# Linear attention and two feed-forward stages on one core: heads laid out in pairs on both halves of the partitions, banks and plan of the work changed

## The chip, the cores and the metric

The kernel runs on one core of a Trainium2 chip. A core has a matrix engine (TensorE, here PE; its weight loads are listed as PEld), a vector engine (VectorE, DVE), an activation engine (ScalarE, ACT), a general engine (GpSimd, POOL) and a queue that issues transfers (SyncE, SP). SBUF is the working memory of 128 partitions; PSUM holds what PE writes, in 8 banks of 512 f32 values a partition. The metric is the device time in microseconds, the median of several runs.

## The reference

Three stages follow one another on 1536 tokens (2 batches of 768) of 384 features (8 heads of 48).

```python
# 1: attention with a decaying state; w is a decay per head and feature, u a bonus
for t in range(S):
    cur = np.einsum('bhd,bhe->bhde', u[None] * kt, vt)
    y[:, :, t] = np.einsum('bhd,bhde->bhe', rt, state + cur)
    state = w[None, :, :, None] * state + np.einsum('bhd,bhe->bhde', kt, vt)
# 2: four experts of 1024 hidden units, all of them run, weighted by p
for e in range(E):
    h = np.maximum(x @ w1[e], 0.0)
    out += p[:, e:e + 1] * (h @ w2[e])
# 3: 2048 hidden units
h = x @ w_in
g = h * (1.0 / (1.0 + np.exp(-1.702 * h)))
return (g @ w_out).astype(np.float32)
```

All arithmetic is f32.

## The kernel before

**Attention** works on 12 groups of 128 tokens (`attention`, L566), six to a batch. Inside a group the decay between two tokens is a quotient of powers, so keys and queries are scaled with tables of powers (`kp` and `rp`, made in `powers`, L493, from `pw`) to `kk` and `rr`. Two heads lie one behind the other on 96 partitions. For even heads the scores are a matmul on the first 48 rows, for odd heads one on all 96 rows with a copy of the keys, `kb`, whose first 48 rows are zeroed by a mask (`b_`, L587). `scores` (L655) is one step for each half of the heads; `mask` copies the later part of them over a diagonal, `at`, that holds the bonus (from `ruk` and `ss`; made on GpSimd by `diag`, L636, and in group 0 half of it on ScalarE by `dact`, L645). `values` (L706) multiplies by the values into `y`, half by half, and adds the carried state `sn`, which `products` (L680) updates from `kc` (keys by token times a table). `high` and `low` write the result as two f32r parts, `xh` and `xl`.

**The feed-forward stages** are 168 units (L752): block 0 (expert 0) 48 of 256 tokens, blocks 1 to 5 (three experts, and the last stage in two halves) 24 each of 512 tokens. A unit takes one chunk of 128 hidden units. Each f32 product is made of three f32r ones: high by high, high by low, low by high. So `up` (L769) is 9 matmuls into one of two banks, ScalarE and DVE read them out into `gh` and `gl` (three buffers each), and `down` (L824) is 9 more into three banks that are kept for 8 units. `end` adds the block's share to `acc`.

**Weights** come in chunks by SP (`load_w`, three buffers) and are split into `wh` and `wl` (`split_w`, 8 buffers each). Those of the last stage arrive as 64-bit numbers and are first made f32 by seven steps (`narrowing`, L145): six on DVE and a sum on GpSimd into one of `NR` = 8 buffers `r`. `narrow_w` (L434) gives all steps of a chunk one due time.

**The order** of all this is written out before the run. `Plan.add` (L60) takes for each step its engine, a cost, a due time, what it reads and writes, and which ring of buffers it takes; `Plan.order` (L84) plays the steps through with these costs and lags (L125 to L142), on each engine the ready step with the lowest due time first, and issues them in the order of their starts. On the chip each engine and the SP queue then keep that order and wait by semaphores. The due times of `up` and `down` make the second follow two units later:

```python
add("pe", 3 * c_mm(P, n, False), 6 * i + d - ..., lambda d=d: up(d), ..., takes=[("up", 2, U)] if d == 0 else ())
add("pe", 3 * c_mm(P, m, False), 6 * i + 12.5 + j + q / 8 - ..., ...)
```

Groups 0 and 1 stand ahead of unit 0, the others between the units of block 0 (L910 to L920). Matmuls called `warm` (L387) fill PE where the plan sees it idle before unit 0. `close` (L923) frees what attention held; from there on the "late" buffers exist.

Of the kernel before, what the change touches and what calls it, by code (L numbers as in the profile page):

```python
# [23 lines left out]
PD = 2 * D  # L24
G = 128
# [8 lines left out]
NR = 8  # L34
# [12 lines left out]
class Plan:  # L47
# [12 lines left out]
    def add(self, eng, cost, due, fn, reads=(), writes=(), takes=(), lag=None):  # L60
        i = len(self.ops)
        deps = set()
# [3 lines left out]
        for ring, size, k in takes:  # L66
            ks = self.rings.setdefault(ring, [])
            if ks:
# [56 lines left out]
LAG = {"dma": 2.6, "pe": 0.1, "dve": 0.1, "act": 0.1, "pool": 0.1, "none": 0.0}  # L125


def c_dve(n, fast=False):
    return (n / 2 if fast else n) / 960 + 0.07


def c_act(n, psum=True):
    return (n + (157 if psum else 224)) / 1400


def c_pool(n):
    return n * 0.0022 + 0.12


def c_mm(m, n, wide=True):  # L140

    return 2 * max(m / 1200, n / 1200) if wide else max(m / 1200, n / 2400)  # L142
# [25 lines left out]
def powers_of(nc, pw, w, most=None):  # L168
# [7 lines left out]
    while m < G:  # L176
        nc.vector.tensor_tensor(
            out=pw[:, :, m + 1:2 * m + 1], in0=pw[:, :, 1:m + 1],
            in1=pw[:, :, m:m + 1].to_broadcast([PD, NP, m]), op=ALU.mult)
# [161 lines left out]
def body(outer: ExitStack, tc: tile.TileContext, wv, cst, msk, dp, rk, tok, wts, wts2, out):  # L341
# [28 lines left out]
    wvs = ac_p.tile([PD, NP, 1], F32, name="wvs")  # L370
    cs = ac_p.tile([P, NCST], F32, name="cs")
    o = 0
    ub = cs[:, o:o + DM]; o += DM
    hm = cs[:PD, o:o + 1]; o += 1
    later = cs[:, o:o + G].bitcast(I32); o += G
    eye = cs[:, o:o + G]; o += G
    own = cs[:PD, o:o + PD]
    dps = ac_p.tile([P, E, NBT], F32, name="dps")
    pw = ac_p.tile([PD, NP, G + 1], F32, name="pw")
    qh = ac_p.tile([PD, NP, 1], F32, name="qh")  # L380
    rp = ac_p.tile([PD, NP, G], F32, name="rp")
    kp = ac_p.tile([PD, NP, G], F32, name="kp")
    wg = ac_p.tile([PD, NP, PD], F32, name="wg")
    tab = ac_p.tile([P, NP, PD], F32, name="tab")
# [14 lines left out]
    def load_const(key, due, t, src):  # L399
        add("dma", 0.1 if key in ("wv", "dp") else 0.5, due, lambda: sp.dma_start(t, src), writes=[key], lag=1.0)  # L400

    def load_group(g, dues):
        def one(i):
            if i == 0:
                T["rk", g] = rk_p.tile([PD, 2, NP, G], F32, tag="rk", name="rk")
                sp.dma_start(T["rk", g], rk[g])
# [6 lines left out]
        for i, k in enumerate(("rk", "tok", "val")):  # L413
            add("dma", 1.1, dues[i], lambda i=i: one(i), writes=[(k, g)], takes=[(k, 2, (k, g))],
                lag=1.0 if g < 2 else None)

    add("dma", 1.65, -9999, lambda: None)
    load_const("wv", -990, wvs.rearrange("p a b -> p (a b)"), wv)


    def load_w(q, due):
        if q < NMOE // 2:
            def fn():
                t = wraw_p.tile([P, 2, CW], F32, tag="w", name="w")
                sp.dma_start(t, wts[q])
                T["raw", q] = t
        else:
            def fn():
                t = wraw_p.tile([P, CW, 2], I32, tag="w", name="w")
                sp.dma_start(t.rearrange("p n t -> p (n t)"), wts2[q - NMOE // 2].bitcast(I32))  # L430
                T["raw", q] = t
        add("dma", 2.2, due, fn, writes=[("raw", q)], takes=[("w", NRAW, ("raw", q))])

    def narrow_w(c, due):  # L434
        k = c - NMOE
        q = NMOE // 2 + k
        load_w(q, due - 40)
        A, M, R = ("cva", k), ("cvm", k), ("r", c)
        tm = lambda: T[M]
        hi = lambda: T["raw", q][:, :, 1]  # L440
        lo = lambda: T["raw", q][:, :, 0]

        steps = narrowing(nc, hi, lo, lambda: T[A], tm, lambda: T[R])
# [14 lines left out]
        add("dve", f, due, first, reads=[("raw", q), "late"], writes=[M], takes=[("cvm", 2, M)])  # L458
        add("dve", f, due, steps[1], writes=[M])
        add("dve", f, due, steps[2], writes=[M])  # L460
        add("dve", l, due, sign, reads=[("raw", q), M], writes=[A], takes=[("cva", 2, A)])
        add("dve", f, due, steps[4], reads=[A], writes=[M])
        add("dve", l, due, steps[5], reads=[("raw", q)], writes=[M])
        add("pool", c_pool(CW), due, sum_, reads=[A, M], writes=[R], takes=[("r", NR, R)])

    def split_w(c, due):
        if c < NMOE and c % 2 == 0:
            load_w(c // 2, due - 20)
# [23 lines left out]

    def powers(half):  # L493
        s = slice(half * HP, (half + 1) * HP)
        qb = qh[:, s].to_broadcast([PD, HP, G])
        add("dve", c_dve(HP * G), -970 + 4 * half, lambda: dve.tensor_tensor(
            out=kp[:, s], in0=pw[:, s, 0:G][:, :, ::-1], in1=qb, op=ALU.mult), reads=["pw"], writes=[("kp", half)])
        add("dve", c_dve(HP * G), -969 + 4 * half, lambda: dve.tensor_tensor(
            out=rp[:, s], in0=pw[:, s, 0:G], in1=qb, op=ALU.mult), reads=["pw"], writes=[("rp", half)])

    def tables(due):

        kt = ac_p.tile([PD, NP, G], F32, name="kt")
        add("pool", 0.85, due, lambda: pool.tensor_tensor(
            out=kt, in0=kp, in1=pw[:, :, G:G + 1].to_broadcast([PD, NP, G]), op=ALU.mult),
            reads=[("kp", 0), ("kp", 1), "pw"], writes=["kt"])

        def turn():
            T["tab_ps"] = ps_at.tile([P, NP, PD], F32, tag="kv", name="tab_ps")
            for p in range(NP):  # L510
                pe.transpose(T["tab_ps"][:, p, :], kt[:, p, :], eye[:PD, :PD])
        add("pe", 0.9, due + 1, turn, reads=["kt", "cs1"], writes=["tab_ps"], takes=[("kv", 1, "tab_ps")])
# [504 lines left out]
```

## Time and profile before

| | us |
|---|---|
| median of 3 runs | 699.15 (699.08 to 701.87) |
| the profiled execution | 702.13 |
| its span, first to last instruction | 700.4 |
| PE busy in it | 678.6 |
| DVE, ACT, POOL busy in it | 369.6, 194.9, 169.9 |

The span is what the engines' instructions cover; the profiled execution's own time is 1.73 us longer. "Busy" counts an engine's instructions from start to end. PE's matmuls overlap, so the start-to-start times in a timeline tell its pace better than its busy time. A row's "idle before" is how long the engine had nothing to do ahead of it, with what released it.

### The profile page before, as it was taken

To read this page: it belongs to the slowest core of one execution; us is meant where nothing else is said; L and a number is where in the kernel's file an instruction comes from. 1 tells how busy PE (TensorE), PEld (TensorE's weight loads), DVE (VectorE), ACT (ScalarE), POOL (GpSimd) and SP (SyncE) were. 2 spreads that over 40 slices of the span, in tenths; PEclk is the share of its full clock that TensorE was granted. 3 is DMA by queue.
4 is the path that set the end of the run, shared out by engine and by line. 5 is a ranking of instruction groups with operands and counts; after the bars stand their busy time and mean duration, and the time that the engine had idled before them with its cause. 6 is when DMAs were issued, how large, how long until landed. Compare 5 with 4: busy or idle time off the path is not lost.

```text
span 700.4 us, 8982 instructions
## 1 busy us (share of the span) xinstructions
PE 678.6 (97%) x3644; PEld 584.1 (83%) x3644; DVE 369.6 (53%) x559; ACT 194.9 (28%) x351; POOL 169.9 (24%) x139
## 2 busy tenths in 40 slices
PE   8979999999999999999999999999799999999996
PEld 7879999999988888878888888887578888888885
DVE  7684554543585224784134764179993345434433
ACT  3432222222421113311113212134324344432331
POOL 6799545620012201223020302042430000000000
PEclk8799999999999999999999999999999999999999
DMA  7766332100252001351002430002100000001001
GB/s 230 238 209 206 89 93 70 46 23 1 81 191 91 0 1 45 136 181 45 1 0 91 145 126 1 0 1 90 46 0 1 1 0 1 1 0 46 18 28 49
DMA packets 12546, 45.90 MB, mean 66 GB/s; under 512 B 2129, under 2 KB 2642, under 8 KB 12498
## 3 DMA queue, kind: packets, MB, share of 16 engines
q1 hardware_dynamic: 12498, 45.26, 19.7%
q8 instruction: 30, 0.49, 0.3%
q14 instruction: 18, 0.15, 0.1%
HBM read 42.87 MB, written 2.38 MB: 65 GB/s over the span
## 4 chain that ended last, share of the span: by engine, by line
PE 82%; DVE 11%; POOL 2%; issue 2%; ACT 1%; DMA 1%; SPq 0%; DVEq 0%; POOLq 0%
PE dn L829 37%; PE up L775 36%; PE sc L661 4%; PE y L714 3%; DVE wl L479 1%; DVE a L154 1%; PE y L718 1%; DVE m L151 1%; DVE m L150 1%; PE kv L684 1%; DVE m L152 1%; DVE gl L794 1%; DVE m L157 1%; DMA tok<-in_tok 1%; POOL sn L695 1%
## 5 line engine op out<-in xcount | busy, mean ns | idle before, releaser
L775 PE MATMUL up<-xh,wh 128*128 128x512 f32 (+1 forms) x504 | 184.8, 367 | 4.0 <-DVE gl L794 2.3
L829 PE MATMUL dn<-gl,wh 128*128 128x512 f32 (+1 forms) x512 | 182.4, 356 | 2.4 <-DVE gl L813 2.4
L829 PE MATMUL dn<-gh,wh 128*128 128x512 f32 (+1 forms) x512 | 182.6, 357 | 1.3 <-DVE tp L855 1.2
L829 PE MATMUL dn<-gh,wl 128*128 128x512 f32 (+1 forms) x512 | 182.1, 356 | 0.0
L775 PE MATMUL up<-xl,wh 128*128 128x512 f32 (+1 forms) x504 | 180.9, 359 | 0.3 <-DVE xl L738 0.3
L775 PE MATMUL up<-xh,wl 128*128 128x512 f32 (+1 forms) x504 | 180.7, 359 | 0.0
L794 DVE SCALAR_TENSOR_TENSOR gl<-up,gh 128x512 fp32r<-128x512 f32 (+1 forms) x120 | 69.8, 582 | 161.0 <-ACT gh L788 160.7
L788 ACT ACTIVATE gh<-up 128x512 fp32r<-128x512 f32 (+1 forms) x120 | 61.5, 513 | 303.8 <-PE up L775 300.0
L775 PEld LDWEIGHTS up<-xh,wh 128*128 128x128 f32 x504 | 95.1, 189 | 19.7 <-DVE gl L794 3.6
L829 PEld LDWEIGHTS dn<-gl,wh 128*128 128x128 f32 x512 | 96.6, 189 | 17.2 <-DVE gl L813 3.0
L829 PEld LDWEIGHTS dn<-gh,wh 128*128 128x128 f32 x512 | 96.6, 189 | 16.7 <-ACT wh L475 1.6
L829 PEld LDWEIGHTS dn<-gh,wl 128*128 128x128 f32 x512 | 96.6, 189 | 13.5
L775 PEld LDWEIGHTS up<-xl,wh 128*128 128x128 f32 x504 | 95.1, 189 | 14.0 <-DVE xl L738 0.5
L775 PEld LDWEIGHTS up<-xh,wl 128*128 128x128 f32 x504 | 94.9, 188 | 13.9
L858 POOL TENSOR_TENSOR acc<-acc,tp 128x512 f32<-128x512 f32 x27 | 38.2, 1424 | 168.7 <-DVE tp L855 168.3
L809 DVE TENSOR_TENSOR gf<-up,sg 128x512 f32<-128x512 f32 x48 | 33.2, 691 | 75.2 <-ACT sg L805 75.2
L159 POOL TENSOR_TENSOR r<-a,m 128x768 f32<-128x768 f32 x16 | 31.5, 1970 | 132.3 <-DVE m L157 77.8
L805 ACT ACTIVATE sg<-up 128x512 f32<-128x512 f32 x48 | 28.7, 598 | 82.3 <-PE up L775 81.9
L813 DVE TENSOR_TENSOR gl<-gf,gh 128x512 fp32r<-128x512 f32 x48 | 33.4, 696 | 22.6 <-ACT gh L788 21.7
L788 ACT ACTIVATE gh<-gf 128x512 fp32r<-128x512 f32 x48 | 30.4, 632 | 41.5 <-DVE gf L809 41.0
L479 DVE TENSOR_TENSOR wl<-w,wh 128x768 fp32r<-128x768 f32 x32 | 35.1, 1098 | 2.5 <-ACT wh L475 1.9
L714 PE MATMUL y<-at,val 128*96 128x128 f32 x192 | 30.3, 288 | 1.1 <-DVE at L664 1.1
(78 smaller groups left out, 545.1 us busy)
## 6 DMA issues: line engine op xcount, KB each, us to landing
w<-in_wts SPq DMA_DIRECT2D x32, 768.0 KB, 4.4
rk<-in_rk SPq DMA_DIRECT2D x12, 384.0 KB, 4.1
tok<-in_tok SPq DMA_DIRECT2D x12, 384.0 KB, 3.8
val<-in_tok SPq DMA_DIRECT2D x12, 384.0 KB, 3.4
pb<-pscr SPq DMA_DIRECT2D x4, 768.0 KB, 4.0
out_t<-tp SPq DMA_DIRECT2D x8, 256.0 KB, 2.0
out_t<-tp SPq DMA_DIRECT2D x2, 128.0 KB, 4.1
cs<-in_cst SPq DMA_DIRECT2D x1, 192.5 KB, 4.1
```

The source lines that it names most:

```text
L159: lambda: pool.tensor_tensor(out=r(), in0=f(a), in1=f(m), op=ALU.add),
L479: dve.tensor_tensor(out=T[L_], in0=src(), in1=T[H_].bitcast(F32), op=ALU.subtract)
L661: pe.matmul(sc[:, j, :], lhsT=a[:n, h // 2, :], rhs=T[RR][:n, h // 2, :], start=True, stop=True)
L714: pe.matmul(y[:, p, :], lhsT=v2[:, h].rearrange("p b d -> p (b d)"), rhs=T["at", g, half][:, h % NP, :], start=hh == 0, stop=first and hh ...
L775: pe.matmul(T[U][:, :n], lhsT=a[:, s], rhs=b, start=d + k == 0, stop=d + k == 4)
L788: act.activation(out=T[GH][:, :n], in_=T[src][:, :n], func=f)
L794: dve.scalar_tensor_tensor(out=T[GL][:, :n], in0=T[U][:, :n], scalar=0.0, in1=T[GH][:, :n].bitcast(F32), op0=ALU.max, op1=ALU.subtract)
L805: act.activation(out=T[SG][:, :n], in_=T[U][:, :n], func=ACTF.Sigmoid, scale=1.702)
L809: dve.tensor_tensor(out=T[GF][:, :n], in0=T[U][:, :n], in1=T[SG][:, :n], op=ALU.mult)
L813: dve.tensor_tensor(out=T[GL][:, :n], in0=T[GF][:, :n], in1=T[GH][:, :n].bitcast(F32), op=ALU.subtract)
L829: pe.matmul(T[dn][:, cols], lhsT=T[a][:, s], rhs=T[b][:, cols], start=first and k == 0, stop=last and k == 2)
L858: pool.tensor_tensor(out=av, in0=av, in1=T[TP][:, :n], op=ALU.add)
```

## The change

Heads lie in pairs at partitions 0 to 47 and 64 to 111, so that tables, keys, queries and state have 112 rows (`PR`); each such load is two DMAs (`by_heads`). The scores of a group are one step: the even head of each pair on the lower half, the odd one on the upper half, in turn, into two banks. `kb`, its mask and `kp` go; the keys use `rp` read backwards. `at` holds even or odd heads instead of the first or last four; groups 0 and 1 make their diagonals wholly on ScalarE, the others two of four. `values` is one step. The state product of group 0, the transposed table and `y` of group 1 take banks of the `down` ring, the scores of group 1 the two `up` banks. Units from block 1 on follow their `up` with `down` three units later, and use two more `up` banks. Narrowing gets 12 buffers, a single buffer for its raw data, and its steps one by one behind units. Unit 0 does its two products with `xh` first. Costs, lags and due times of the plan are new.

```diff
-NR = 8
+NR = 12
+HS = 64
+PR = HS + D
-    def add(self, eng, cost, due, fn, reads=(), writes=(), takes=(), lag=None):
+    def add(self, eng, cost, due, fn, reads=(), writes=(), takes=(), lag=None, after=()):
-        deps = set()
+        deps = {j for k in after for j in self.wrote[k]}
...
-LAG = {"dma": 2.6, "pe": 0.1, "dve": 0.1, "act": 0.1, "pool": 0.1, "none": 0.0}
+LAG = {"dma": 2.6, "pe": 0.18, "dve": 0.12, "act": 0.12, "pool": 0.1, "none": 0.0}
...
+    def by_heads(engines, t, src):
+        engines[0].dma_start(t[:HS], src[:HS])
+        engines[1].dma_start(t[HS:], src[D:])
...
-                sp.dma_start(T["rk", g], rk[g])
+                by_heads((sp, sp), T["rk", g], rk[g])
...
-    add("dma", 1.65, -9999, lambda: None)
-    load_const("wv", -990, wvs.rearrange("p a b -> p (a b)"), wv)
+    add("dma", 0.75, -9999, lambda: None)
+    add("dma", 0.1, -990, lambda: by_heads((sp, act), wvs.rearrange("p a b -> p (a b)"), wv), writes=["wv"], lag=1.0)
...
-        add("dve", f, due, first, reads=[("raw", q), "late"], writes=[M], takes=[("cvm", 2, M)])
-        add("dve", f, due, steps[1], writes=[M])
...
+            lambda due, after: add("dve", f, due, first, reads=[("raw", q), "late"], writes=[M],
+                                   takes=[("cvm", 1, M)], after=after),
+            lambda due, after: add("dve", f, due, steps[1], writes=[M], after=after),
...
-            load_w(c // 2, due - 20)
+            load_w(c // 2, due - (60 if c < 8 else 20))
...
+    kp = rp[:, :, ::-1]
...
+        add("pool", 1.2, due, lambda: pool.memset(kcs, 0.0), writes=["kcs"])
...
-            def b_(s=s, i=i):
-                if i == 0:
-                    new(KB, [PD, NP, G])
-                act.activation(out=T[KB][:, s], in_=T[KK][:, s], func=ACTF.Copy, scale=hm)
...
-                on_act = 2 if g == 0 else 0
+                on_act = 4 if g < 2 else 2
...
-                for j in (0, 2, 1, 3):
-                    h = half * NP + j
-                    a, n = (T[KB], PD) if h % 2 else (T[KK], D)
-                    pe.matmul(sc[:, j, :], lhsT=a[:n, h // 2, :], rhs=T[RR][:n, h // 2, :], start=True, stop=True)
+            for p in range(NP):
+                for half in range(2):
+                    rows = slice(half * HS, half * HS + D)
+                    pe.matmul(T[sck[half]][:, p, :], lhsT=T[KK][rows, p, :], rhs=T[RR][rows, p, :], start=True, stop=True)
...
+            kv, kv_tag = ("kv", g), "sc0" if g else "dn2"
...
+        y_tag = "dn1" if g == 1 else "y"
...
+        deep = blk > 0
+        far = deep and i % 4 > 1
+        ups = [(d, ks) for ks in ((0, 2), (1,)) for d in range(3)] if i == 0 else [(d, (0, 1, 2)) for d in range(3)]
...
-                T[U] = ps_up.tile([P, 512], F32, tag="up", name="up")
+                T[U] = (late["up"] if far else ps_up).tile([P, 512], F32, tag="up", name="up")
...
-                add("pe", 3 * c_mm(P, m, False), 6 * i + 12.5 + j + q / 8 - (5.5 if i == len(units) - 1 else 0),
+                add("pe", 3 * c_mm(P, m, False), 6 * i + (18.5 if deep else 12.5) + j + q / 8 - (5.5 if i == len(units) - 1 else 0),
...
-    router(0)
+    router(-500)
...
+        late["raw"] = ctx.enter_context(tc.tile_pool(name="raw64", bufs=1))
+        late["up"] = ctx.enter_context(tc.tile_pool(name="ps_up2", bufs=2, space=PSUM))
...
+    def hand_over(chunks, u, v):
+        each = (v - u) / len(chunks)
+        for n, c in enumerate(chunks):
+            for m in range(6):
+                steps_at.setdefault(int(u + each * (n + m / 8.5)), []).append((c, m))
+
+    hand_over(range(NMOE, NMOE + NR), e0 + 6, k0)
+    hand_over(range(NMOE + NR, NCH), k0 + 1, k0 + 18)
...
+        for cn, m in steps_at.get(i, ()):
+            if m == 0:
+                load_w(NMOE // 2 + cn - NMOE, 6 * i - 40)
+                steps_of[cn] = narrow_w(cn)
+            steps_of[cn][m](6 * i + 12, [("up", i)])
```

## Rows read from the trace of the kernel before

**Rows 1.** The page, part 1: each engine's busy time, share, instructions.

```profile
PE 678.6 (97%) x3644; PEld 584.1 (83%) x3644; DVE 369.6 (53%) x559; ACT 194.9 (28%) x351; POOL 169.9 (24%) x139
```

**Rows 2.** Chain of waits around 212 us: start, length, engine, tile, line, count.

```profile
212.01 0.68 PE up L775 x3
```

**Rows 3.** Timeline of PE around a group's scores: start, length, line, tile, shapes.

```profile
87.62 0.28 PE L829 MATMUL dn<-gl,wh 128*128 128x256 f32 x1
87.74 0.28 PE L829 MATMUL dn<-gh,wl 128*128 128x256 f32 x1
87.95 0.71 PE L661 MATMUL sc<-rr,kk 48*128 48x128 f32 x4
88.59 0.71 PE L661 MATMUL sc<-rr,kb 96*128 96x128 f32 x4
...
89.26 0.28 PE L775 MATMUL up<-xl,wh 128*128 128x256 f32 x1
```

**Rows 4.** Timeline of PE from group 0's values to unit 0.

```profile
12.58 3.73 PE L714 MATMUL y<-at,val 128*96 128x128 f32 x16 [1.07 <-DVE at L664]
16.24 1.22 PE L661 MATMUL sc<-rr,kk 48*128 48x128 f32 x4
...
20.70 1.49 PE L684 MATMUL kv<-val,kc 128*96 128x96 f32 x8
21.98 2.39 PE L391 MATMUL warm<-acc 128*128 128x128 f32 x10
24.17 1.06 PE L714 MATMUL y<-at,val 128*96 128x128 f32 x4
...
29.29 0.36 PE L775 MATMUL up<-xh,wh 128*128 128x256 f32 x1
```

**Rows 5.** Stretches: length, busy PE, PEld, DVE, ACT, POOL, clock, DMA share, GB/s.

```profile
8.00:12.00 4.00, 2.31 (x16) 1.82 (x16) 3.96 (x7) 1.78 (x5) 3.75 (x4) 0.97 1.00 296
12.00:24.00 12.00, 11.42 (x50) 10.47 (x51) 7.97 (x15) 4.58 (x11) 8.70 (x11) 0.50 0.53 153
29.29:54.00 24.71, 20.14 (x164) 18.61 (x162) 19.57 (x35) 9.50 (x18) 23.06 (x18) 1.00 0.74 244
54.00:80.00 26.00, 25.54 (x209) 24.45 (x208) 15.48 (x30) 6.73 (x17) 22.71 (x22) 1.00 0.50 165
80.00:184.00 104.00, 104.00 (x864) 100.95 (x863) 48.20 (x98) 26.09 (x67) 34.24 (x32) 1.00 0.16 43
290.00:310.00 20.00, 19.54 (x86) 15.87 (x86) 16.93 (x21) 4.47 (x7) 6.24 (x4) 1.00 0.44 157
480.00:525.00 45.00, 38.42 (x162) 29.37 (x161) 43.74 (x55) 15.49 (x24) 15.39 (x8) 1.00 0.11 38
```

**Rows 6.** Timelines of ACT and POOL in the head.

```profile
9.14 0.68 ACT L646 ACTIVATE at<-cs,ss 128x128 f32<-128x128 f32 x2
...
16.07 2.05 POOL L638 TENSOR_TENSOR at<-ss,cs 128x512 f32<-128x512 f32 x2
...
22.33 2.78 POOL L677 TENSOR_TENSOR kc<-tok,tab 128x384 f32<-128x384 f32 x1 [2.98 <-issue]
```

**Rows 7.** Timeline of the SP queue at the start.

```profile
1.18 0.41 SPq L406 DMA_DIRECT2D rk<-in_rk  x1
```

**Rows 8.** Timeline of PE at the change to block 4.

```profile
490.25 0.50 PE L775 MATMUL up<-xh,wh 128*128 128x512 f32 x1 [1.30 <-DVE gl L794]
```

**Rows 9.** POOL's groups in 480 to 525 us: count, busy, mean ns.

```profile
L159 POOL TENSOR_TENSOR r<-a,m 128x768 f32<-128x768 f32 x5 | 10.3, 2069 | 26.3 <-DVE m L157 26.3
```

**Rows 10.** Timeline of DVE there: steps of the narrowing.

```profile
475.73 0.95 DVE L157 SCALAR_TENSOR_TENSOR m<-w,m 128x768 f32<-128x768 uint32 x1
476.60 0.55 DVE L150 TENSOR_SCALAR m<-w 128x768 int32<-128x768 int32 x1
477.19 2.08 DVE L151 TENSOR_SCALAR m<-m 128x768 f32<-128x768 f32 x1
```

**Rows 11.** Timeline of POOL beside it.

```profile
476.83 2.02 POOL L159 TENSOR_TENSOR r<-a,m 128x768 f32<-128x768 f32 x1 [4.49 <-DVE m L157]
```

More of the change, by code (lines that the diff above doesn't have):

```diff
@@ L67, in add @@
             ks = self.rings.setdefault(ring, [])
-            if ks:
+            if ks and ks[-1] in self.wrote:
                 deps.add(self.wrote[ks[-1]][0])
@@ L514, in tables @@
+        add("pe", 0.9, due + 1, turn, reads=["kt", "cs1"], writes=["tab_ps"], takes=[("dn1", 1, "tab_ps")])
+        add("act", c_act(DM), due + 2, lambda: act.activation(
+            out=tab.rearrange("p a b d -> p a (b d)")[:, :, :PR], in_=T["tab_ps"], func=ACTF.Copy),
             reads=["tab_ps"], writes=["tab"])
+        add("pool", 1.2, due, lambda: pool.memset(kcs, 0.0), writes=["kcs"])
         add("pool", 0.95, -500, lambda: pool.tensor_tensor(
-            out=wg, in0=pw[:, :, G:G + 1].to_broadcast([PD, NP, PD]), in1=times(own, PD, NP), op=ALU.mult),
@@ L517, in tables @@
-            reads=["pw", "cs1"], writes=["wg"])
+            out=wg, in0=pw[:, :, G:G + 1].to_broadcast([PR, NP, PD]), in1=times(own, PR, NP), op=ALU.mult),
+            reads=["pw", "own"], writes=["wg"])
     flag = const.tile([1, 1], I32, name="flag")
@@ L578, in attention @@
             n = (s.stop - s.start) * G
-            tabs = [("kp", j) for j in range(2) if s.start <= j * HP < s.stop]
             tabr = [("rp", j) for j in range(2) if s.start <= j * HP < s.stop]
@@ L644, in attention @@
+                add("pool" if on_act < NP else "none", c_pool((NP - on_act) * G) if on_act < NP else 0.0, d + 3, diag, reads=[SS, *((*SS, i) for i in ((0, NP) if g < 2 else (0,))), "cs1"],
+                    writes=[(*at, 0)], takes=[("at%d" % half, 2, at)])
                 for j in range(NP - on_act, NP):
-                    def dact(at=at, half=half, j=j):
-                        act.activation(
-                            out=T[at][:, j, :], in_=eye, func=ACTF.Copy, scale=T[SS][:, half * NP + j, :])
@@ new lines, in attention, with scores @@
+                    add("act", 0.3, d + 3, dact, reads=[SS, *((*SS, i) for i in ((0, NP) if g < 2 else (0,))), "cs1", at],
+                        writes=[(*at, j)])
+        sck = [("sc", g, half) for half in range(2)]
+        spare = g == 1
+        on_act = 4 if g < 2 else 2
+        def scores():
+            for half in range(2):
+                T[sck[half]] = (ps_up if spare else ps_at).tile(
+                    [P, NP, G], F32, tag="up" if spare else f"sc{half}", name="sc")
+            for p in range(NP):
+                for half in range(2):
+                    rows = slice(half * HS, half * HS + D)
+                    pe.matmul(T[sck[half]][:, p, :], lhsT=T[KK][rows, p, :], rhs=T[RR][rows, p, :], start=True, stop=True)
@@ L668, in attention, with mask @@
+        add("pe", 4 * c_mm(P, G), due["sc"][0], scores, reads=[KK, RR], writes=sck,
+            takes=[("up", 2, k) if spare else (f"sc{half}", 1, k) for half, k in enumerate(sck)])
+        for half in range(2):
+            at = ("at", g, half)
+            def mask(at=at, half=half):
+                dve.copy_predicated(T[at], times(later, P, NP), T[sck[half]])
             add("dve", c_dve(NP * G), due["mask"][half], mask,
-                reads=[sck, at, (*at, 0), *((*at, j) for j in range(NP - on_act, NP))], writes=[(*at, "m")])
+                reads=[sck[half], at, (*at, 0), *((*at, j) for j in range(NP - on_act, NP))], writes=[(*at, "m")])
@@ L686, in own_ @@
             def own_():
-                new(("sn", g + 1), [PD, NP, PD])
-                dve.tensor_tensor(out=T["sn", g + 1], in0=T[kv], in1=times(own, PD, NP), op=ALU.mult)
-            add("pool", c_pool(DM), due["kc"], by_token, reads=[tk_, "tab"], writes=[KC], takes=[("kc", 1, KC)])
-            add("pe", 4 * c_mm(PD, PD), due["kv"], products, reads=[KC, vl_], writes=[kv], takes=[("kv", 1, kv)])
-            add("dve", c_dve(DM), due["kv"] + 1, own_, reads=[kv, "cs1"], writes=[("sn", g + 1)],
+                new(("sn", g + 1), [PR, NP, PD])
@@ L693, in attention @@
+                dve.tensor_tensor(out=T["sn", g + 1], in0=T[kv], in1=times(own, PR, NP), op=ALU.mult)
+            add("pool", c_pool(DM), due["kc"], by_token, reads=[tk_, "tab", "kcs"], writes=[KC], takes=[("kc", 1, KC)])
+            add("pe", 4 * c_mm(PD, PD), due["kv"], products, reads=[KC, vl_], writes=[kv], takes=[(kv_tag, 1, kv)])
+            add("dve", c_dve(DM), due["kv"] + 1, own_, reads=[kv, "own"], writes=[("sn", g + 1)],
                 takes=[("sn", 2, ("sn", g + 1))])
@@ L941, in body @@
             split_w(c, 6 * i - 8)
-        for cn in narrow_at.get(i, ()):
-            narrow_w(cn, 6 * i - 20)
         if 0 < blk < E and t0 == 0 and c % 8 == 0:
```

247 lines of the change are left out of this document (118 added, 129 removed).

## The prediction

> **What bounds the kernel now.** I read the page first, then busy time by stretch, then TensorE's own timeline where a stretch fell short. The page says that TensorE (PE) is busy 97% of the span [rows 1], so the first question is whether that time is a floor. Nearly all of it is: three matmuls of 512 columns follow one another in 0.68 us, 0.227 us each [rows 2], those of 256 columns every 0.12 us [rows 3]. The program has 120 units of 18 matmuls at 512 columns and 48 units of 18 at 256, none of which the change removes: 120 x 18 x 0.227 + 48 x 18 x 0.12 = 594 us. The remaining 106 us of the span of 700.4 are what can move, and the stretches show where:
>
> - the head: the first matmul of unit 0 starts at 29.29 us [rows 4];
> - attention that PE runs between the units, mainly in 29 to 184 us;
> - idle PE: 24.71 - 20.14 = 4.6 us in 29.29 to 54 us, and 45.00 - 38.42 = 6.6 us in 480 to 525 us. In 80 to 184 us there is none [rows 5].
>
> So a stall that goes is worth its length wherever PE is the last to finish a stretch, and elsewhere nothing.
>
> **Scores in pairs.** Before, a half of the heads is one run: two matmul instructions (the two passes of an f32 matmul) for each of two even heads on 48 rows, then as many on 96 rows. Without the run the second of the `up` matmuls behind it would start two steps of 0.12 after the `dn` at 87.74, at 87.98; it starts at 89.26. One half costs 1.28 us, a group 2.56. The four 48-row passes start at 87.95 and the 96-row ones at 88.59, so eight passes take eight steps of about 0.11 (0.89; the shape of kk's and kb's runs is the same) and the other 0.39 are three changes of shape, 0.13 each: into 48 rows, to 96, and back to 128 [rows 3]. That a change from 48 to 96 rows costs anything, though both lie in the same array, says that PE works a 48-row matmul on a part of its rows in a mode of its own.
>
> After, all 16 passes have 48 rows, alternating between partitions 0 and 64 and between two banks, in one run per group. The switches fall to two (0.26). No row shows matmuls on different halves together, so three bounds: they overlap, 8 x 0.11 + 0.26 = 1.15 us; they follow one another, 16 x 0.11 + 0.26 = 2.04; each change of half costs a switch as well (7 x 0.13 more), 2.95. Saved per group: 1.41, 0.52 or -0.39, and for the ten groups 2 to 11 14.1, 5.2 or -3.9 us. I take the first, because the switch in the rows is the sign of a mode that leaves the other half free.
>
> The Trainium skill, TensorEngine Tiling (Array Packing), section Theoretical Speedup, puts a contraction of at most 64 rows at up to twice the speed, and its section Key Properties says that tiles load weights and multiply in parallel. By it the saving is the 14.1 us; by the rows alone, which show only one half in use, it is the 5.2. No run here shows the rule yet.
>
> The values, the state products and the keys keep their counts. `kb` on ScalarE goes (one activation a group), and ScalarE takes four diagonal activations of 0.34 us from GpSimd [rows 6]: lighter than the idle ScalarE has, as it is busy 26 of 104 us there [rows 5], so nothing on the path. The halves of `y` are now one block that waits for both masks; in 80 to 184 us neither mask is late.
>
> **The head.** Before, the chain on PE from 12.58 us on is: `y` of group 0 (3.7 us), scores of group 1 (16.24 to 20.70, 4.5 us at a granted clock of 0.50, the 1.2 GHz level), its state product (1.3), 2.2 us of warm-up matmuls that only fill a wait, then `y` of group 1 (from 24.17) [rows 4, 5]. The new order puts the diagonals of groups 0 and 1 on ScalarE: 16 x 0.34 = 5.4 us [rows 6], instead of GpSimd, where group 1's two took 2.05 us and began at 16.07 behind other work. Group 0's eight take 2.7 us and end with its masks at about the old 12.6, so its `y` is not earlier. But `kb` is no longer waited for and the two groups have banks of their own, so the scores of group 1 can stand before that `y`, in PE's wait: the 4.5 us leave the chain. With group 1's diagonals done by about 16 us the wait under the warm-up matmuls goes, 2.2 us. Against that `y` of group 1 comes earlier into the slow clock (24 passes at twice 0.11: up to 2.6 us more), and the keys' load is two issues on SP instead of one, 0.41 us each [rows 7]. I take 4.5 + 2.2 - 0.8 - 0.4 = 5.5 us gained. Bounds: 6.7 + 2.6 = 9.3 if the clock is up from the start, so that `y` of group 0 is faster too, nothing if ScalarE's 5.4 us of diagonals take over as the chain. Unit 0 may also begin before its low parts are there, 0.3 us or so, inside this error. The weights of units 0 to 7 now go ahead of the loads of groups 2 and 3. In 12 to 24 us the DMA engines were busy 53% [rows 5], since the queue on SP stood behind a buffer that was not free; the weights fill that gap, so I take nothing, and if they delay group 2, the next paragraph's stall stays.
>
> The tables and products on 112 partitions instead of 96 take the same time where it goes by columns; the state product's 16 more weight columns are at most a sixth of its 1.3 us in the head, and the clearing of `kcs` is one operation on GpSimd. Both stand beside other work after the head, and inside its bounds in it.
>
> **The early stall.** In 29.29 to 54 us GpSimd is busy 23.06 of 24.71 us and DVE 19.57 [rows 5]: PE's 4.6 us are waits for them. GpSimd loses one of two diagonals a group (1.0 us of the 2.05 for a pair [rows 6]), DVE nothing much, and both are asked to keep up with a PE that begins earlier. Also the second `kc` at 22.33 waited 2.98 us for the product before it [rows 6], which the head now runs earlier. I take half: 2.5 us; bounds 0 and 4.6. What is late next here is GpSimd again.
>
> **Narrowing step by step, 12 slots, four banks.** In 480 to 525 us DVE is busy 43.74 of 45 us [rows 5]. 162 matmuls there would need 162 x 0.227 = 36.8 us: 8.2 us are lost, in waits for DVE such as the 1.30 at 490.25 [rows 8]. GpSimd forms the sums of five chunks in that stretch [rows 9]. A chunk is four short steps of 0.55 us on DVE and two of 0.95, 4.1 us, and a short step that meets GpSimd's sum takes 2.08 instead (477.19, beside the sum at 476.83 [rows 10, 11]): 5.6 us. Twelve slots move four of the eight late chunks to where DVE is half idle; the other four come one in 17/4 units of 18 x 0.227 = 4.1 us, about 17 us apart, so 2.6 in such a stretch instead of five. That takes 2.4 x 5.6 = 13.4 us off DVE: some 30 us of work in the 37 that the matmuls need. With a unit more between `up` and `dn`, and two more banks for `up`, a burst may last 4 us longer before PE sees it. I take 7.2 of the 8.2 as gained, and bound it by 0 (the same steps under other units stall PE elsewhere) and 8.2. The same for the stretch around 308 us: 0.4. In the steady stretches the deeper order neither adds nor removes matmuls, and its cost is nothing as long as a unit's results are read out within its 4.1 us, as they are before. The single staging buffer lets a chunk load only after the one before is narrowed; of the 22 us between chunks (5.5 units) some 9 are left for it, and a late one would hold DVE, not PE, for the length of four banks.
>
> **The sum.** 14.1 + 5.5 + 2.5 + 7.2 + 0.4 = 29.7 us. The profiled execution took 702.13 us (span 700.4 and 1.73 around it): 672.4. The median of the runs is 2.98 below that execution, so 669.5 us.
>
> **Rivals.**
>
> - The pairs do not overlap: 29.7 - 8.9 = 20.8 gained, 678.4 us. For it: the rows show no two matmuls at once. Against: the mode of their own.
> - Each change of half costs a switch: 18 us less gained, 687.5. For it: 0.13 at every change of shape seen. Against: shape and mode stay the same here.
> - ScalarE's diagonals become the head's chain, or the early stretch stays bound by GpSimd: 5.5 + 2.5 less, 677.5. For it: GpSimd is full.
> - The narrowing only moves its stalls: 7.6 less, 677.1. For it: the work is the same. Against: the steps no longer come in a row, and four banks cover a burst.
> - Slower: the early stretch starves PE so that its clock falls. In 8 to 12 us PE stood idle for 1.7 of 4 us, and in the 12 us that followed the granted clock was 0.50, the 1.2 GHz level [rows 5]. If the units beside groups 2 to 5 ran so, the 45.7 us that PE is busy in 29.29 to 80 us (20.14 and 25.54 [rows 5]) would double: 669.5 + 45.7 = 715. It decides where waits as long as those of 8 to 12 us come back in the early stretch. For it: PE asks for more there, from a GpSimd that is full. Against: before, 4.6 us of waits in that stretch left the clock at 1.00, and the engines that bound it get less to do.
> - It does not do what it says, the planner's order undoing one part with another: within 3.5 us of before.
>
> **How the numbers follow.** Chances: forecast 0.62 (its own range 663 to 676, from the head's and the stalls' bounds), no overlap 0.17, a switch at each change 0.05, ScalarE or GpSimd 0.05, narrowing 0.05, clock 0.04, nothing 0.02. The range of 661 to 689 us reaches down to a head at its best bound with no stall left, and up past the dearest scores. Faster by over 0.5% (3.5 us, about what this kernel's runs tell from nothing): 0.94; within it 0.02; slower 0.04.
>
> **What would show it.** Scores: one run of 16 passes a group, its cost near 1.15, 2.04 or 2.95 us between the neighbours. Head: unit 0's first `up` 5 us earlier, or as much sooner as the work moved behind it allows, with group 1's scores before group 0's `y`. Early: PE idle in the 25 us behind unit 0 about 2 us. Late: DVE under 80% around the change to block 4 and PE idle about 1 us. The forecast is wrong if the floor of 594 us changes, if steady stretches of 512 columns show idle PE, or if the score run costs over 2 us.

## The result and the profile after

The changed kernel takes 676.61 us (675.80 to 677.81), the one before, on the same chip, 700.51 (699.08 to 702.36): a ratio of 0.966 [0.962, 0.969] (the interval in brackets is the 95% one). The profiled execution took 677.41 us, its span is 675.6. The page and the stretches answer to [rows 1] and [rows 5]:

```profile
PE 663.2 (98%) x3658; PEld 574.7 (85%) x3658; DVE 356.4 (53%) x560; ACT 201.3 (30%) x390; POOL 156.9 (23%) x136
```

Stretches of the kernel after (length, then busy PE, PEld, DVE, ACT, POOL, granted clock, DMA share, GB/s):

```profile
8.00:12.00 4.00, 3.19 (x18) 2.95 (x19) 2.37 (x7) 1.10 (x4) 2.48 (x3) 0.54 1.05 286
12.00:24.00 12.00, 12.00 (x88) 11.50 (x88) 7.38 (x17) 7.08 (x20) 8.21 (x13) 0.73 0.90 258
25.69:54.00 28.31, 25.47 (x217) 23.46 (x217) 23.64 (x39) 13.68 (x35) 27.18 (x24) 1.00 0.90 266
54.00:80.00 26.00, 26.00 (x238) 25.48 (x236) 16.76 (x36) 9.25 (x28) 17.73 (x19) 1.00 0.56 159
80.00:184.00 104.00, 104.00 (x899) 101.61 (x898) 51.52 (x105) 31.92 (x83) 29.08 (x30) 1.00 0.22 67
290.00:310.00 20.00, 20.00 (x90) 16.58 (x89) 6.68 (x10) 2.99 (x5) 1.84 (x1) 1.00 0.12 41
480.00:525.00 45.00, 45.00 (x200) 37.30 (x199) 31.16 (x43) 16.84 (x29) 8.06 (x5) 1.00 0.16 53
```

The last stretch now holds 200 matmuls instead of 162, the one at 80 us 899 instead of 864. In 25.69 to 54 us GpSimd (POOL) is as full as before.

To split the gain I went along PE from start to start: a matmul of 512 columns counts 0.227 us, one of 256 columns 0.12, what lies between beyond that is a stall, and runs of other shapes (scores, values, state products) count whole, with what they delay before and behind them. Both sums close on the span.

| us | before | after | gain | predicted |
|---|---|---|---|---|
| scores, 20 halves (one of before's in the head) | 25.5 | 12.8 | 12.8 | 14.1 |
| head up to unit 0, without that half | 28.0 | 25.7 | 2.3 | 5.5 |
| stalls up to 100 us | 5.9 | 4.6 | 1.3 | 2.5 |
| stalls behind 100 us | 9.3 | 0.2 | 9.1 | 7.6 |
| values and state products | 31.3 | 32.2 | -0.9 | 0 |
| units | 594.2 | 594.2 | 0 | 0 |
| rest | 6.1 | 6.0 | 0.1 | 0 |
| span | 700.35 | 675.62 | 24.7 | 29.7 |

**Scores.** PE's timeline around one group's run, which answers to [rows 3]:

```profile
79.28 0.28 PE L859 MATMUL dn<-gl,wh 128*128 128x256 f32 x1
79.40 0.28 PE L859 MATMUL dn<-gh,wl 128*128 128x256 f32 x1
79.61 1.16 PE L676 MATMUL sc<-rr,kk 48*128 48x128 f32 x16
80.70 0.39 PE L803 MATMUL up<-xh,wh 128*128 128x256 f32 x1
80.93 0.28 PE L803 MATMUL up<-xl,wh 128*128 128x256 f32 x1
```

One run of 16 passes per group, 1.09 us from its first start to the next `up`. The starts of the single passes, from the trace's records:

```
79.613 79.619 | 79.827 79.833 | 79.938 79.944 | 80.049 80.057 | 80.161 80.168 | 80.273 80.279 | 80.384 80.391 | 80.497 80.503
```

The two passes of a pair start 6 to 8 ns apart and a pair follows a pair every 0.111 us, the step of one pass alone. The other cost is at the ends: the first pass starts 0.09 us late and the second pair 0.10, the next `up` and the one behind it 0.10 each. That is 8 x 0.111 + 0.19 + 0.20 = 1.28 us a group, where one half had cost that before. The starts of the half in [rows 3] show where its 0.39 went:

```
kk 87.951 88.165 88.276 88.388 | kb 88.590 88.803 88.915 89.026 | up 89.057 89.258 89.375
```

The change into 48 rows costs 0.09 and 0.10 us, the change from 48 to 96 rows 0.09 and 0.10 again. Back to the 128 rows of `up` costs nothing: the first `up` starts 0.08 us early and the second 0.08 late.

**Head.** PE's timeline, which answers to [rows 4]:

```profile
10.79 1.94 PE L391 MATMUL warm<-acc 128*128 128x128 f32 x8
12.71 2.08 PE L676 MATMUL sc<-rr,kk 48*128 48x128 f32 x16
14.72 2.50 PE L391 MATMUL warm<-acc 128*128 128x128 f32 x10
17.01 2.69 PE L734 MATMUL y<-at,val 128*96 128x128 f32 x16
19.54 0.93 PE L705 MATMUL kv<-val,kcs 128*112 128x96 f32 x8
20.31 1.75 PE L391 MATMUL warm<-acc 128*128 128x128 f32 x14
21.90 0.60 PE L734 MATMUL y<-at,val 128*96 128x128 f32 x4
...
25.70 0.36 PE L803 MATMUL up<-xh,wh 128*128 128x256 f32 x1
```

Group 1's scores stand ahead of group 0's `y`, as predicted, and unit 0 starts 3.6 us earlier. The warm-up matmuls did not go: 24 of them stand in two waits, ahead of each `y`. What these waits are for is on DVE and ScalarE: the last sum `ss` and the diagonals of group 0 with the second mask behind them, then group 1's diagonals and its second mask:

```profile
10.51 0.35 DVE L631 TENSOR_REDUCE ss<-ruk 128x4 f32<-128x192 f32 x1 [1.10 <-POOL ruk L625]
10.90 2.45 ACT L660 ACTIVATE at<-cs,ss 128x128 f32<-128x128 f32 x8 [8.26 <-DVE ss L631]
14.11 0.72 DVE L684 COPY_PREDICATED at<-cs,sc 128x512 f32<-128x512 int32 x1
15.09 2.45 ACT L660 ACTIVATE at<-cs,ss 128x128 f32<-128x128 f32 x8 [1.32 <-DVE ss L631]
20.98 0.74 DVE L684 COPY_PREDICATED at<-cs,sc 128x512 f32<-128x512 int32 x1
```

In the kernel before, group 0's two masks were these; the first half of `y` followed the first one at 12.58 [rows 4]:

```profile
11.81 0.72 DVE L664 COPY_PREDICATED at<-cs,sc 128x512 f32<-128x512 int32 x1
13.49 0.71 DVE L664 COPY_PREDICATED at<-cs,sc 128x512 f32<-128x512 int32 x1
```

### The profile page after: what moved, and what is told of

Same layout as the page of the kernel before. It is cut to its first block, busy times and chain, and to the rows that moved or that the text cites. A ratio compares the mean times of both kernels' runs of the same rounds, so it can differ in the third digit from the quotient of the medians.

```text
span 675.6 us, 9093 instructions
## 1 busy us (share of the span) xinstructions
PE 663.2 (98%) x3658; PEld 574.7 (85%) x3658; DVE 356.4 (53%) x560; ACT 201.3 (30%) x390; POOL 156.9 (23%) x136
## 4 chain that ended last, share of the span: by engine, by line
PE 93%; DVE 3%; DMA 1%; POOL 1%; issue 1%; SPq 1%; ACT 0%; DVEq 0%; POOLq 0%
PE up L803 43%; PE dn L859 43%; PE y L734 3%; PE sc L676 1%; PE y L738 1%; DMA rk<-in_rk 1%; PE kv L705 1%; DVE rr L605 0%; DVE wl L492 0%; DMA pscr<-pn 0%; DVE xl L758 0%; DVE at L684 0%; DVE xl L755 0%; DVE ss L631 0%; POOL tn L722 0%
## 5 line engine op out<-in xcount | busy, mean ns | idle before, releaser
L161 POOL TENSOR_TENSOR r<-a,m 128x768 f32<-128x768 f32 x16 | 29.8, 1863 | 224.9 <-DVE m L159 224.9
L888 POOL TENSOR_TENSOR acc<-acc,tp 128x512 f32<-128x512 f32 x27 | 39.7, 1478 | 103.2 <-DVE tp L885 102.8
L843 DVE TENSOR_TENSOR gl<-gf,gh 128x512 fp32r<-128x512 f32 x48 | 33.6, 701 | 24.7 <-ACT gh L818 23.3
L734 PE MATMUL y<-at,val 128*96 128x128 f32 x192 | 28.6, 278 | 0.0
```

The source lines that it names most:

```text
L161: lambda: pool.tensor_tensor(out=r(), in0=f(a), in1=f(m), op=ALU.add),
L734: pe.matmul(y[:, p, :], lhsT=v2[:, 2 * p + hh].rearrange("p b d -> p (b d)"), rhs=T["at", g, hh][:, p, :], start=hh == 0, stop=first and h ...
L843: dve.tensor_tensor(out=T[GL][:, :n], in0=T[GF][:, :n], in1=T[GH][:, :n].bitcast(F32), op=ALU.subtract)
L888: pool.tensor_tensor(out=av, in0=av, in1=T[TP][:, :n], op=ALU.add)
```

## The experiments

**Is it the order of the pairs that makes them overlap?** The same 16 passes, all of the lower half first:

```diff
-            for p in range(NP):
-                for half in range(2):
+            for half in range(2):
+                for p in range(NP):
```

> The changed kernel with one thing undone: a group's 16 score passes no longer alternate between the two halves of the rows; all of the lower half come first, then all of the upper half. Still one run, 48 rows each, two banks. Theory (passes overlap only where neighbours in the order lie on different halves): a group's run costs 16 x 0.111 + 0.38 = 2.16 us instead of 1.28, 0.88 more for each of ten groups, and up to 2 us more in the head, where the clock is at its lower level: 685 to 687.5 us against 676.6. Rival (the saving came from there being fewer changes of shape, not from overlap): the run stays at 1.28 us and the time at 676.6.

683.92 us (682.72 to 684.41), 0.977 [0.972, 0.981] of before instead of 0.966. The run, and the starts of its passes:

```profile
81.75 1.71 PE L676 MATMUL sc<-rr,kk 48*128 48x128 f32 x16
83.39 0.38 PE L803 MATMUL up<-xh,wh 128*128 128x256 f32 x1
```
```
lower 81.752 81.966 82.077 82.189 82.301 82.412 82.524 82.636
upper 82.307 82.520 82.632 82.743 82.855 82.967 83.078 83.190
```

The run takes 1.64 us instead of 1.09, the ten groups 18.2 instead of 12.8. One half alone steps at 0.111 too. PE did not wait for the end of the lower half: the upper half's first pass starts 6 ns after the fifth lower one, and the last three lower passes run beside upper ones. So in these rows each half has its own stream, the order decides how long both are fed, and my 2.16 us (no overlap at all) was too dear by 0.34. The rival, no change at all, is out. The ten groups make 5.4 of the 7.3 us between the two medians, and unit 0 starts 1.0 us later (26.70); the rest is open.

**Which part carries the late gain?** Each of three undone alone; `down` two units behind `up` instead of three (which takes the two further `up` banks too), a chunk's steps handed over in one unit, 8 slots instead of 12:

```diff
-        deep = blk > 0
+        deep = False
```
```diff
-                steps_at.setdefault(int(u + each * (n + m / 8.5)), []).append((c, m))
+                steps_at.setdefault(int(u + each * n), []).append((c, m))
```
```diff
-NR = 12
+NR = 8
```

> The changed kernel with the deeper order undone: from block 1 on, the second matmuls of a unit follow two units after the first again, and only two banks take the first ones. The narrowing stays step by step with 12 slots. Theory (the narrowing's work was moved and spread, and that alone removed the 9.3 us of stalls behind 300 us): stalls there stay under 1.5 us, 676.6 to 678. Rival (the deeper order hid the bursts): the stalls come back in part, 4 to 9 us, 681 to 686.

> The changed kernel with the spreading of the steps undone: all six steps of a chunk's narrowing stand behind the same unit; the 12 slots, the chunks' distances and the deeper order stay. A chunk is 4.1 to 5.6 us of VectorE in a row against a unit of 4.1. Theory (the deeper order alone covers one such burst): stalls behind 300 us under 1.5 us, 676.6 to 678. Rival (the spreading is what removed the stalls): 4 to 9 us come back, 681 to 686.

> The changed kernel with 8 instead of 12 buffers for narrowed chunks: eight chunks are narrowed ahead of block 4 and eight in its first 17 units, one in 2.1 units (8.7 us), as dense as before the change. Theory (the move of four chunks took the load off): VectorE is over 90% busy around 460 to 505 us and 3 to 8 us of stalls come back there, 680 to 685. Rival (spread steps and the deeper order hide even the dense narrowing): under 1.5 us of stalls, 676.6 to 678. The single staging buffer may hold a chunk's steps back here, as its load takes 4.2 us of the 3.6 that are left for it.

676.15 (674.92 to 677.23), 675.38 (675.24 to 676.15) and 679.21 us (678.68 to 680.08). Late stalls (those behind 100 us): 0.24, 0.24 and 2.59 us. The first two parts cost nothing when taken away, as their theories had it. 8 slots cost 2.4 us of stalls, behind 511 us, and some 3 us of time: less than the theory's 3 to 8, more than the rival's. DVE is busy 33.52 of 45 us in 460 to 505, not over 90%; it is full only later, 47.04 of 55 us in 505 to 560. Then the first two together, and all three:

> The down units go in two units later again and the first half of a chunk's narrowing is spread as before, both together; the 12 slots of the up banks (four narrowing chunks later) stay. PE's stalls behind 54 us were 9.32 us before the change, 0.23 after it, 0.24 with either of the two undone alone, 2.59 with 8 slots. Theory: the 12 slots alone carry the late gain, so the stalls behind 54 us stay under 1.5 us and the time within 1.5 us of the changed kernel's (676 to 678). Rival: the deep order and the spreading each suffice for the other, and with both gone 4 to 9 us of late stalls come back: 681 to 686.

> As the run before it, and 8 slots for the up banks instead of 12 as well: what is left of the change is the paired scores, the own banks of the first groups and the shared power table. Theory: the three undone parts are together the whole late gain, so 7 to 9 us of stalls behind 54 us return, most of them between 480 and 550 us: 684 to 686. Rival: the paired scores, which give DVE the same work in less time, make the late stretch tighter than it was before: over 10 us of late stalls, 687 or more. If under 4 us come back (under 681), the refitted plan's costs did a share that none of these parts holds.

677.19 us (676.54 to 678.72) with 0.64 of late stalls, as the theory had it: 12 slots without these two are enough. But with all three undone 678.81 (677.76 to 681.04), and only 2.82 us of late stalls: neither theory nor rival, but the third branch. DVE's and PE's work in 480 to 525 us of that run:

```profile
480.00:525.00 45.00, 44.49 (x192) 35.43 (x191) 37.98 (x53) 14.31 (x24) 9.25 (x5) 1.00 0.25 88
```

Like before [rows 9] it forms five chunks there, at 8 slots, and yet DVE is busy 38 us, not 43.74. Groups of DVE in 440 to 560 us show it (count | busy us, mean ns), first in the kernel before, then with all three undone:

```profile
L150 DVE TENSOR_SCALAR m<-w 128x768 int32<-128x768 int32 x6 | 7.4, 1228 | 1.9 <-POOL r L159 1.9
L154 DVE SCALAR_TENSOR_TENSOR a<-w,m 128x768 int32<-128x768 int32 x6 | 6.5, 1087 | 0.1
L151 DVE TENSOR_SCALAR m<-m 128x768 f32<-128x768 f32 x6 | 6.4, 1066 | 0.1
L152 DVE TENSOR_SCALAR m<-m 128x768 int32<-128x768 int32 x6 | 4.9, 812 | 0.2
```
```profile
L156 DVE SCALAR_TENSOR_TENSOR a<-raw,m 128x768 int32<-128x768 int32 x8 | 7.7, 957 | 0.2
L152 DVE TENSOR_SCALAR m<-raw 128x768 int32<-128x768 int32 x8 | 5.2, 654 | 0.5 <-DMA raw<-in_wts 0.5
L154 DVE TENSOR_SCALAR m<-m 128x768 int32<-128x768 int32 x8 | 4.5, 558 | 0.2
L153 DVE TENSOR_SCALAR m<-m 128x768 f32<-128x768 f32 x8 | 4.5, 558 | 0.2
```

The same steps are short now: all six of a chunk take 4.26 us of DVE, before 5.70 (both sums over the six groups of the window by their count; in the kernel after it is 4.26 too). Before, 14 of the 96 steps overlapped a GpSimd sum, often the next chunk's first ones that of the chunk ahead [rows 10, 11]; now none does. Two candidates for what keeps them apart, each put back on top of the three: the early due time with two buffers of `m` and `a`, and the old costs of the plan.

```diff
-            steps_of[cn][m](6 * i + 12, [("up", i)])
+            steps_of[cn][m](6 * i - 20, [])
...
-                                   takes=[("cvm", 1, M)], after=after),
+                                   takes=[("cvm", 2, M)], after=after),
```
```diff
-LAG = {"dma": 2.6, "pe": 0.18, "dve": 0.12, "act": 0.12, "pool": 0.1, "none": 0.0}
+LAG = {"dma": 2.6, "pe": 0.1, "dve": 0.1, "act": 0.1, "pool": 0.1, "none": 0.0}
...
-    return n * 0.0022 + 0.16
+    return n * 0.0022 + 0.12
```

> From the kernel with all three parts undone (its stalls behind 54 us are 2.82 us, not the 7 to 9 expected), the steps of a chunk's narrowing are also asked for 20 ahead of the unit again instead of behind a unit's up products, with two buffers of m and of a as before; the costs of the plan stay the new ones. Theory: what the three parts don't hold is the meeting of a chunk's first short steps with GpSimd's sum of the chunk before it (before: 1.89 and 2.08 us instead of 0.55), which the handing over behind a unit and the single buffers prevent: such steps of 1.9 us or more come back, DVE in 480 to 525 us rises from 37.98 to over 41 of 45 us, and the late stalls grow to 6 us or more (682 to 686). Rival: the costs that the plan was refitted with hold the rest: late stalls stay under 4 us, 678 to 680.

> From the kernel with all three parts undone, the plan's costs (the lag behind each engine, and the cost functions of DVE, ScalarE, GpSimd and of a matmul) are those of the kernel before; the handing over of the narrowing steps behind a unit stays. Theory (the steps' meeting with the sum, not the costs, is the rest): late stalls stay at 2 to 4 us. Rival (the costs hold the rest): 6 us or more of late stalls, 682 or more. The head may move by 1 to 2 us either way, since its order comes from the same costs.

679.00 us (678.53 to 679.47), late stalls 1.26, DVE 33.84 in 480 to 525 us and 39.18 in 460 to 505, a chunk 4.50 us: the theory missed, the chunks stay apart (2 of the 96 steps meet a sum), though six of them fall into 440 to 560 us as before. 677.48 (675.52 to 679.44), late stalls 1.07: the costs don't hold it either, and there are even fewer stalls than the 2 to 4 us of that theory. What all these kernels share and the one before lacks is, among other things, one staging buffer for the 64-bit chunk, by which the next chunk can land only when the last step that reads it is done. The run with the early due time shows it at work, as its steps are asked for early and still wait (DVE's last step of one chunk, GpSimd's sum, DVE's first step of the next chunk):

```profile
459.34 0.95 DVE L159 SCALAR_TENSOR_TENSOR m<-raw,m 128x768 f32<-128x768 uint32 x1
461.23 1.86 POOL L161 TENSOR_TENSOR r<-a,m 128x768 f32<-128x768 f32 x1 [3.82 <-DVE wl L492]
464.58 0.56 DVE L152 TENSOR_SCALAR m<-raw 128x768 int32<-128x768 int32 x1 [0.68 <-DMA raw<-in_wts]
```

The next load is issued at 460.31, 0.02 us behind the last step that reads the buffer, and takes 4.2 us. At all fifteen changes of chunk in that run 4.1 us or more lie between the last step of one and the first of the next, and a sum takes 1.8 to 2.5; in the kernel before it was 1.2 us or less at nine of the fifteen. That the stalls come back with more staging buffers was not tried.

**Is the head short of its forecast because of the clock?** The changed kernel once more, and with eight filler matmuls inside group 0's scores, where PE stands idle; two more kernels make the diagonals of groups 2 and 3 on ScalarE, against the early stalls:

```diff
             for p in range(NP):
+                for _ in range(4 if g == 0 and p in (0, HP) else 0):
+                    warm()
```
```diff
-                on_act = 4 if g < 2 else 2
+                on_act = 4 if g < 4 else 2
```

> The changed kernel unchanged, beside the next three on the same chip: 676.6 us, its runs some 2 us apart, as in its first four. In four executions with the same order ahead of unit 0 the first matmul of unit 0 started at 25.7, 24.8, 23.5 and 22.4 us, the earlier the sooner the granted clock was back at 1.00.

> The changed kernel with eight more warm-up matmuls: four ahead of the first and four ahead of the second half of group 0's scores, where TensorE waits 1.16 and 1.08 us for VectorE. Theory (the head fell 3 us short of the forecast because these waits let the clock fall to its lower level at 8 to 18 us, and the work behind them runs at half pace): the clock stays at 1.00 from 8 us on, unit 0 starts at 22.4 us as in the one execution that had it so, and the median falls by 2 to 3 us, to 674. Rival (the level in 8 to 18 us comes from elsewhere, or the loads hold the head in any case): clock and time as before, 676.6, or 0.4 us worse for two more changes of shape each.

> The changed kernel with the diagonals of groups 2 and 3 wholly on ScalarE too. Theory (behind unit 0 GpSimd is the bound, 27.2 of 28.3 us busy): it loses four operations of 0.6 us there, and of the 4.6 us of early stalls 1 to 2.4 go: 674.5 to 675.5. Rival (VectorE, at 23.6 of 28.3 us, holds those stalls, as the 1.44 us one behind a gl shows): within 0.5 us of the changed kernel.

> The two edits before this one together, as a version that may beat the changed kernel: if both theories hold 672 to 673 us, if both rivals do 676.6.

The changed kernel again: 676.75 us (674.42 to 678.75), 0.964 [0.962, 0.967]. With fillers 675.00 (673.68 to 676.40), 0.962 [0.960, 0.964]: the intervals overlap, so it is no better for certain. The head did as the theory said, but the profiled execution without fillers had the same clock there, so the fillers are not shown to be the reason. Stretches of the changed kernel's first profiled execution, of its second, and of the one with fillers:

```profile
12.00:16.00 4.00, 4.00 (x26) 3.50 (x26) 3.02 (x8) 2.68 (x10) 3.65 (x5) 0.50 1.04 357
26.00:30.00 4.00, 3.20 (x28) 2.48 (x26) 3.25 (x8) 2.50 (x5) 3.84 (x5) 1.00 1.04 338
30.00:54.00 24.00, 21.96 (x188) 20.70 (x188) 20.08 (x32) 11.19 (x30) 23.03 (x20) 1.00 0.88 253
```
```profile
12.00:16.00 4.00, 3.43 (x37) 3.31 (x38) 2.89 (x7) 2.51 (x9) 3.78 (x5) 1.00 1.06 355
26.00:30.00 4.00, 3.85 (x38) 3.52 (x38) 4.00 (x4) 1.87 (x6) 3.92 (x5) 1.00 1.05 305
30.00:54.00 24.00, 20.16 (x164) 19.26 (x162) 17.36 (x30) 9.87 (x25) 19.36 (x18) 0.93 0.89 254
```
```profile
12.00:16.00 4.00, 4.00 (x44) 3.88 (x43) 2.62 (x7) 3.25 (x12) 3.68 (x8) 1.00 1.03 351
26.00:30.00 4.00, 4.00 (x26) 3.55 (x25) 4.00 (x5) 0.47 (x2) 3.82 (x4) 0.50 1.02 294
30.00:54.00 24.00, 22.12 (x192) 21.32 (x193) 17.60 (x30) 11.19 (x30) 20.85 (x18) 0.95 0.88 253
```

The first line of each is the head. At 0.50 (the 1.2 GHz level) unit 0 starts at 25.70 us, at 1.00 (2.4 GHz) at 22.78 and, with fillers, 22.02. But the spans are 675.6, 675.3 and 674.6: in these executions a unit 0 that starts earlier waits more, and the clock then falls behind it (0.50 from 38.7 to 42.1 us in the second, from 25.5 to 32.3 with fillers). With fillers, `up` waits 1.63 us at 22.5 for `xh`, which ScalarE could not write before DVE's `xl`, and the loss up to 100 us rises from 4.6 to some 7 us; part of that is the pace at 0.50, where a 256-column matmul takes a step of 0.21 us and not 0.12. It is not always all lost. Five of the runs above (8 slots, the two parts undone, `down` two units behind, all three undone, a chunk in a row) issue the same instructions in the same order as the changed kernel up to block 1. Unit 0 starts 0.9, 1.1, 2.2, 2.3 and 3.3 us earlier in them than at 25.70; the first `up` of block 1, at 176.68 us in the first execution of the changed kernel, starts 0.2 us earlier, 0.1 later, then 1.1, 2.0 and 2.0 earlier. In the second execution unit 0 is 2.9 us earlier and block 1 0.4 later.

The diagonals on ScalarE: 680.95 us (676.76 to 686.61), with fillers as well 681.05 (676.65 to 684.67). Both expectations missed; by the medians it is slower by some 4 us, and the runs lie 8 to 10 us apart, those of the changed kernel 4.3. Two things show in the profiled execution of the first, at 686.61 its slowest. One is the clock:

```profile
30.00:40.00 10.00, 8.44 (x65) 8.23 (x66) 7.32 (x12) 3.61 (x9) 4.74 (x3) 0.81 1.02 281
40.00:54.00 14.00, 14.00 (x115) 13.88 (x112) 10.64 (x12) 7.54 (x21) 13.20 (x14) 0.88 0.66 187
54.00:80.00 26.00, 21.73 (x168) 20.61 (x168) 17.91 (x35) 5.92 (x18) 14.38 (x15) 0.87 0.55 157
```

It was at 0.50 three times between 26.9 and 64.5 us, for 17.1 us together, where the kernel after has 1.00 throughout. PE is busy 69.60 of the 76.93 us from unit 0 to 100 us, so 7.3 us idle, in the kernel after 71.47 of 74.31, 2.8 idle. The longer steps at 0.50, summed over that stretch against those at 1.00, make some 7 us by my estimate; the two spans differ by 9.2. The other thing is DVE:

```profile
49.88 4.68 DVE L492 TENSOR_TENSOR wl<-w,wh 128x768 fp32r<-128x768 f32 x1
54.48 1.47 DVE L605 TENSOR_TENSOR rr<-rk,rp 112x512 f32<-112x512 f32 x1
```

A split `wl` that takes 0.95 us alone takes 4.68 here, beside a GpSimd that is busy 13.2 of the 14 us from 40 to 54; `gl` stands behind it and `up` stalls 3.66 us at 54.1. That the relief let GpSimd's next work start elsewhere, under another step of DVE, is a guess. How much of either the faster executions have is open, as one was profiled: the fastest, 676.76 us, had a granted clock of 0.996 over its span and the slowest 0.983, but one of 681.05 had 0.996 too.

## Why the prediction was right or wrong

- **The time is inside the range, the mechanisms are in the main those of the likeliest case.** 676.61 us is 7.1 us above the forecast of 669.5 and 0.6 above the 663 to 676 of that case. Three rivals' times, 677.1, 677.5 and 678.4, lie nearer to it, so the time alone tells nothing between them; the rows do. The terms fell 5.0 us short (24.7 against 29.7), the other 2.2 us are the profiled execution's place: 2.98 us above the median before, which I took off again, 0.80 after. That was chance.
- **Scores: right in mechanism, 1.3 us too much.** The pairs overlap as fully as they can. The failed step is "three changes of shape, 0.13 each": the half before had two that cost anything, 0.19 each, into 48 rows and from 48 to 96, and none back to 128. The run after has two again, 0.19 and 0.20, where I counted 0.26 for both. So a group saves 8 x 0.111 + 0.39 = 1.28, not 1.41. The Trainium skill, TensorEngine Tiling (Array Packing), sections Theoretical Speedup and Key Properties, has the double speed and the independent loads and matmuls; the trace agrees (6 ns inside a pair, 0.111 between pairs). The rivals "no overlap" and "a switch at each change of half" are out, the second also by the experiment on the order, where each half kept its step.
- **Head: right order, 3.2 us too much.** Two steps failed. One is that group 0's diagonals "end with its masks at about the old 12.6": at 12.53 only the first mask ended before, the second at 14.20, and the second half of `y` waited for it. Now `y` is one block that waits for both, and the second mask ends at 14.83. The other is "with group 1's diagonals done by about 16 us the wait under the warm-up matmuls goes": they end at 17.54, and the second mask starts on DVE only at 20.98, behind the state product's `own` at 20.51, which waits for PE. The clock adds to it: at 0.50 the scores and the fillers keep PE until 17.01, 2.2 us beyond the mask.
- **What the head is worth.** In the execution at 1.00 the head gains 29.29 - 1.28 - 22.78 = 5.2 us on the one profile of the kernel before, which was at 0.50. That it comes near the 5.5 is luck: the 5.5 was worked out at 0.50, and for a clock that is up from the start the prediction had 9.3. I also took the head for a gain of the whole kernel, and it is so only in part: of a unit 0 that starts 0.9 to 3.3 us earlier than in the first execution, between nothing and 2.0 us were left at block 1. The rival in which waits behind unit 0 bring the clock down did happen in part, for 3.4 us in the second execution, 6.8 with fillers and 17.1 with the diagonals on ScalarE, not for the 45.7 us of a whole stretch.
- **Early stall: half of what was taken, 1.3 us for 2.5.** GpSimd stays as full as before (27.18 of 28.31 us), as the prediction put it. Whether it is the bound is open: the largest wait left, 1.44 us at 51.2, is `up` behind `gl`, which DVE reaches late because `rr` before it took 2.13 us (0.69 at 11.97), and taking diagonals off GpSimd did not shorten the stretch.
- **Narrowing: near in size (9.1 for 7.6), wrong in reason.** "Twelve slots move four of the eight late chunks" is enough by itself, as the run with the other two undone shows, but not needed: at 8 slots 1.1 to 2.8 us of stalls remain of 9.3. The missed step is that I priced a chunk at 5.6 us after as before; it is 4.3, as its steps no longer run beside GpSimd's sums. I saw the single staging buffer only as a possible delay. In one run the wait for it keeps the steps apart, but no run has the rest of the change without it, so which part holds the gain stays open. The deeper order, the four banks and the spreading, to which I gave a part, bring nothing that a run could tell.
- **State products: 0.8 us lost**, 112 weight columns for 96: 0.71 us a group for 0.62. I had bounded it in the head and counted nothing behind it.

## What to carry to other kernels

The 48-row matmuls pay off in pairs, on both halves of the rows and in two banks, and in full only when the program's order alternates the halves: with the loops swapped, 0.55 of the 1.28 us saved per group are lost again. Before crediting a rearrangement with a gain, undo its parts together as well as one by one: here three parts looked like the cause, two were worth nothing, and most of the gain outlived all three. A gain in a slow start is not yet a gain of the kernel: follow it to a later place, here the first matmul of block 1, and see what is left.

## What the runs showed that was not expected

- Short DVE steps on 768 columns take 0.55 us alone and up to 2.08 beside a sum on GpSimd [rows 10, 11]; a `wl`, with two inputs, took 2.60 us beside the sum at 487.04 in the kernel after, and 4.68 us in the worst case above. The Trainium skill, GPSIMD Engine Reference, section Specifications, has such contention for DVE instructions with two SBUF inputs or in a two-port mode; the `wl` rows agree, and which mode the short steps ran in no row shows. A chunk cost 1.4 us more in the kernel before.
- The same program got clocks of 0.50 and of 1.00 in 12 to 16 us in two executions, unit 0 started 2.9 us apart, and the spans differ by 0.3 us.
- A load split in two at partition 64 can issue slower as well as twice: group 0's keys took 0.57 and 0.58 us on SP, 1.15 together, the whole load 0.41 [rows 7], so 0.7 us more and not the 0.4 of the prediction. Later such issues vary, 0.34 to 0.70 us a part in the head.

```profile
1.36 0.57 SPq L404 DMA_DIRECT2D rk<-in_rk  x1
1.99 0.58 SPq L405 DMA_DIRECT2D rk<-in_rk  x1
```
